# Group 0 made tile by tile in a set order with loads split over two queues, and key normalisers ahead of the next group's norm

## The chip, the cores and the metric

One core of one Trainium2 chip. The metric is the device time of one launch in microseconds (us). One profiled execution of each kernel gives a trace; a page and several views (chain of waits, timeline, windows, DMA) are read from it. "Clock" is the share of full speed that TensorE was granted, as the trace records it (1.00 is full, 0.50 half). The span of a trace is 1.8 to 1.9 us shorter than the time of its run.

## The reference, cut to what matters

```python
xn = (x - mean(x)) / sqrt(var(x) + 1e-5)                 # x: 2048 x 512
q, k, v = split(xn @ wqkv)                               # 32 heads of 16
pq, pk = q @ w_phi[h], k @ w_phi[h]                      # per head, 16 x 16
phi_q = concat(softmax(pq), softmax(-pq));  phi_k = concat(softmax(pk), softmax(-pk))
kv = sum_s phi_k[s]^T v[s];  z = sum_s phi_k[s]
A = ((phi_q @ kv) / (phi_q @ z + 1e-6)) @ wo
B = mish(xn @ w1 + b1) @ w2                              # 512 -> 1792 -> 512
out = x + A + B
```

kv is a sum over all tokens, so all keys come before any attention output. w_phi is folded into the key and query weights at the start.

## The kernel before: the parts that the change and the argument touch

The tokens run in four groups of four tiles of 128. In each group TensorE (PE) makes keys (pk), values (pv), queries (pq), seven pairs of hidden blocks (ph) and the kv sums (pkv). VectorE (DVE) sums and inverts the exponentials of the keys (ss, rk), scales the values with them (v), adds the kv sums up (kvacc), and makes the norm of the next group (st, mv, xn). ScalarE (ACT) does exponentials and Mish. POOL is GpSimd; it makes the root (rstd) of the norms after group 0. "follow" ties an instruction behind the last one of the same name in the scheduler; what is not tied, the scheduler orders. PSUM is the memory in which PE leaves its results; its buffers here are three large and two small ones, so PE waits where none is free.

```python
ps_kq = tile_pool(name="ps_kq", bufs=3, space=PSUM)   # "big": pk, pq, ph, pkv, fold
ps_v  = tile_pool(name="ps_v",  bufs=2, space=PSUM)   # pv
# ... loads, before
nc.sync.dma_start(xgs[0][:], x_g[0])
nc.scalar.dma_start(wk_raw[:], wqkv_v[:, :, D:2*D])
nc.sync.dma_start(wv[:], wqkv_v[:, :, 2*D:3*D])
nc.scalar.dma_start(Wsrc[:], wphi_v)
nc.scalar.dma_start(wq_raw[:], wqkv_v[:, :, 0:D])
# ... the norm of a group: only the statistics are tied
follow("dve", nc.vector.bn_stats(st[:], xg[:, t, :]))
nc.vector.bn_aggr(mv[:, t, :], st[:])
nc.vector.tensor_scalar(out=xn[:], in0=xg[:, t, :], ...)     # L190
nc.sync.dma_start_transpose(out=xnT[:, t], in_=xn[:])        # groups 1 to 3
# ... the loop
for g in range(NG):
    if g == 0: ...
    else:
        ek0 = k_pair(xnT, 0); ek1 = k_pair(xnT, 1)
        v0, vfin = v_pair(xnT, 0)
    vfin(ek0)                                  # ss, rk, v of tiles 0 and 1
    q_pair(g, xnT, 0); q_pair(g, xnT, 1)
    h_pair(xnT, acts[g], 0)
    v1, vfin = v_pair(xnT, 1)
    vfin(ek1)                                  # ss, rk, v of tiles 2 and 3
    if g + 1 < NG:
        xnTs[g + 1], _ = stage_ln(g + 1)       # the next group's norm
    for fp in range(1, 4): h_pair(xnT, acts[g], fp)
    stage_kvacc(g, parts)                      # 2 x pkv on PE, 2 x kvacc on DVE
    for fp in range(4, 7 if g + 1 < NG else 6): h_pair(xnT, acts[g], fp)
```

The softmax here doesn't subtract the row's maximum and nothing guards it: scores larger than these inputs give would overflow.

## Time and profile before

| | before |
|---|---|
| time, median of 3 runs | 196.7 us (196.59 to 196.71) |
| profiled run, its span | 197.05 us, 195.2 us |
| first hidden pair | 23.28 |
| keys of groups 1, 2, 3 start | 38.99, 71.03, 95.37 |
| length of group 1, group 2 | 32.04, 24.34 |
| half clock of TensorE | 53.28 to 60.11 |

All positions are us from the start of the span. Group lengths are the distance between the first key matmuls (pk) of neighbours in PE's timeline. The clock row is from the trace's records of the granted clock. Most of the lines themselves stand in the prediction; these two, for the start, do not (DVE's first look at x, and the first hidden pair; in brackets the idle time before it and what ended it):

```profile
4.59 1.29 DVE L182 BATCH_NORM_STATS2 st<-xg 128x6 f32<-128x512 bf16 x2 [3.35 <-DMA xg<-in_A_x_dram]
```
```profile
23.28 1.89 PE L366 MATMUL ph<-xnT,w_sb 128*128 128x512 bf16 x8 [0.40 <-ACT eqT L357]
```

### The profile page before, as it was taken

The page shows a single profiled execution, that of the slowest core. Times are in us where ns is not written, and L with a number is a line of the kernel's source. Part 1 is how long each engine was busy: PE and PEld are TensorE (multiplying, and loading weights), DVE is VectorE, ACT ScalarE, POOL GpSimd, SP SyncE. Part 2 cuts the span into 40 slices and gives each one's busy share as a digit, 9 for nine tenths or more (in the row PEclk, how much of TensorE's full clock was granted, in tenths as well). Part 3 has the DMA queues.
Part 4 walks back from the last instruction along what each step waited for, and adds up shares of the span by engine and source line. Part 5 has one row for each costly group of instructions (what it writes and reads, how often), then busy time and mean ns, then how long its engine had stood idle before and what let it go on. Part 6 is the DMA issues. An engine that isn't in the chain of part 4 may idle for free.

```text
span 195.2 us, 2791 instructions
## 1 busy us (share of the span) xinstructions
PE 181.2 (93%) x1034; PEld 90.7 (46%) x1051; DVE 119.0 (61%) x233; ACT 107.9 (55%) x175; POOL 14.0 (7%) x35
## 2 busy tenths in 40 slices
PE   7779999999189999999999999999999999999992
PEld 2355446444034644446444464445555555555440
DVE  1948999364894203982039864897666677766600
ACT  3578976598704479974799855343322222333311
POOL 3200410202110000110001100000000000000000
PEclk9999999999958999999999999999999999999999
DMA  6999302619300013000000000138322632222220
GB/s 192 381 403 386 151 0 55 125 59 197 108 0 0 3 27 81 0 0 3 0 0 0 0 3 0 27 81 165 55 69 66 164 81 57 54 54 57 54 81 27
DMA packets 24233, 15.93 MB, mean 82 GB/s; under 512 B 16284, under 2 KB 23196, under 8 KB 24220
## 3 DMA queue, kind: packets, MB, share of 16 engines
q1 hardware_dynamic: 22636, 14.69, 27.4%
q10 hardware_dynamic: 1584, 1.07, 1.7%
q8 instruction: 8, 0.13, 0.3%
q14 instruction: 5, 0.04, 0.1%
HBM read 9.98 MB, written 2.10 MB: 62 GB/s over the span
## 4 chain that ended last, share of the span: by engine, by line
PE 75%; ACT 7%; DVE 7%; DMA 5%; issue 2%; SPq 2%; POOL 1%; ACTq 0%; DVEq 0%; POOLq 0%
PE ph L366 25%; PE po L453 22%; PE po L462 6%; PE pv L283 6%; PE pk L265 4%; PE pkv L326 4%; DMA Wsrc<-in_A_w_phi_dram 4%; PE pq L348 4%; PE pnd L390 4%; SPq L200 2%; ACT ek L274 1%; ACT ek L273 1%; ACT act L377 1%; DMA xnT<-xn 1%; DVE ss L297 1%
## 5 line engine op out<-in xcount | busy, mean ns | idle before, releaser
L366 PE MATMUL ph<-xnT,w_sb 128*128 128x512 bf16 x224 | 51.8, 386 | 0.4 <-ACT eqT L357 0.4
L453 PE MATMUL po<-w_sb,act 128*128 128x512 bf16 x216 | 51.2, 379 | 0.4
L377 ACT ACTIVATE act<-ph,b1f 128x512 bf16<-128x512 f32 x56 | 35.5, 684 | 27.4 <-PE ph L366 27.4
L366 PEld LDWEIGHTS <-w_sb 128*128 128x128 bf16 x224 | 22.2, 100 | 27.1 <-issue 2.9
L471 ACT CAST y<-po 128x512 bf16<-128x512 f32 x16 | 9.4, 586 | 44.4 <-PE po L462 44.4
L453 PEld LDWEIGHTS <-act 128*128 128x128 bf16 x224 | 21.3, 98 | 22.3
L297 DVE TENSOR_REDUCE ss<-ek 128x64 f32<-128x1024 bf16 x16 | 18.7, 1211 | 19.1 <-ACT ek L274 19.0
L422 DVE TENSOR_TENSOR on<-pnd,wd 128x512 f32<-128x512 f32 x32 | 20.6, 686 | 1.7
L283 PE MATMUL pv<-wv,xnT 128*128 128x512 bf16 x59 | 16.4, 408 | 5.0 <-DVE v L305 4.6
L305 DVE TENSOR_TENSOR v<-pv,rk 128x1024 bf16<-128x1024 f32 x16 | 18.3, 1188 | 0.0
L462 PE MATMUL po<-wo_sb,oT 128*128 128x512 bf16 x63 | 16.4, 379 | 0.1
L357 ACT ACTIVATE eqT<-pq 128x1024 bf16<-128x1024 f32 x16 | 15.1, 1040 | 0.7 <-PE pq L348 0.6
L182 DVE BATCH_NORM_STATS2 st<-xg 128x6 f32<-128x512 bf16 x16 | 10.4, 672 | 8.1 <-DMA xg<-in_A_x_dram 8.1
L348 PE MATMUL pq<-xnT,wqp 128*128 128x512 bf16 x64 | 14.5, 379 | 0.0
L265 PE MATMUL pk<-wkp,xnT 128*128 128x512 bf16 x61 | 14.3, 379 | 0.2
L407 DVE TENSOR_TENSOR td<-ds 128x64 f32<-128x64 f32 x16 | 3.6, 225 | 16.4 <-ACT ds L403 16.3
L283 PEld LDWEIGHTS <-xnT 128*128 128x128 bf16 x64 | 6.5, 103 | 13.0 <-issue 6.6
L390 PE MATMUL pnd<-kvm,eqT 128*128 128x144 bf16 x128 | 11.3, 226 | 0.5 <-DVE on L422 0.3
L390 PEld LDWEIGHTS <-eqT 128*128 128x128 bf16 x128 | 9.0, 98 | 5.9 <-DVE on L422 2.4
L313 POOL CAST v<-rk 128x64 bf16<-128x64 f32 x16 | 7.0, 458 | 64.5 <-DVE rk L303 64.5
L429 DVE TENSOR_TENSOR o_t<-on 128x512 bf16<-128x512 f32 x16 | 11.1, 692 | 0.5
L338 DVE TENSOR_TENSOR kvacc<-pkv,kvacc 128x544 f32<-128x544 f32 x6 | 4.3, 725 | 9.9 <-PE pkv L326 9.9
(63 smaller groups left out, 150.1 us busy)
## 6 DMA issues: line engine op xcount, KB each, us to landing
xg<-in_A_x_dram SPq DMA_DIRECT2D x8, 512.0 KB, 4.1
out_dram<-y SPq DMA_DIRECT2D x16, 128.0 KB, 2.1
w_sb<-in_B_w_dram SPq DMA_DIRECT2D x2, 896.0 KB, 9.9
w_sb<-in_B_w_dram SPq DMA_DIRECT2D x1, 1792.0 KB, 12.9
wk_raw<-in_A_wqkv_dram ACTq DMA_DIRECT2D x1, 512.0 KB, 5.1
wv<-in_A_wqkv_dram SPq DMA_DIRECT2D x1, 512.0 KB, 6.0
wq_raw<-in_A_wqkv_dram ACTq DMA_DIRECT2D x1, 512.0 KB, 10.1
wo_sb<-in_A_wo_dram SPq DMA_DIRECT2D x1, 512.0 KB, 13.5
```

The source lines that it names most:

```text
L265: pe(nc.tensor.matmul(pk[:, tt, :], lhsT=xnT[:, 2 * pr + tt, kt, :], rhs=wkp[:, kt, :], start=(kt == 0), stop=(kt == KT - 1),))
L283: nc.tensor.matmul(pv[:], lhsT=xnT[:, 2 * pr + tt, kt, :], rhs=wv[:, kt, :], start=(kt == 0), stop=(kt == KT - 1),)
L297: nc.vector.reduce_sum(ss[:], ek[:, :, tt, :].rearrange("p s (h e) -> p s h e", e=DH), axis=AX.X,)
L305: nc.vector.tensor_tensor(out=v12[:, :, :, 0:DH], in0=pvs[tt][:] .rearrange("p (o h e) -> p o h e", o=1, e=DH) .to_broadcast([P, 2, NH, DH ...
L348: pe(nc.tensor.matmul(pq[:, jj, :], lhsT=wqp[:, kt, j * P : (j + 1) * P], rhs=xnT[:, :, kt, :], start=(kt == 0), stop=(kt == KT - 1),))
L357: follow("act", nc.scalar.activation(eqT[:, sl, gs], pq[:], ACT.Exp, scale=sign))
L366: nc.tensor.matmul(ph[:, ff, :], lhsT=w1_sb[:, kt, f * P : (f + 1) * P], rhs=xnT[:, :, kt, :], start=(kt == 0), stop=(kt == KT - 1),)
L377: nc.scalar.activation(act[:, f, :], ph[:, ff, :], ACT.Mish, bias=b1f[:, f : f + 1])
L390: nc.tensor.matmul(pnd[:, j // 2, (j % 2) * 144 : (j % 2) * 144 + 144], lhsT=eqT[:, pl * 4 + j, tok0 : tok0 + P], rhs=kvm[:, pl * 4 + j], ...
L422: nc.vector.tensor_tensor(out=on[:, pl], in0=nds[pl][:, :, :, 0:DH], in1=wd[:, pl, :, :, None].to_broadcast([P, 2, 16, DH]), op=ALU.mult,)
L453: nc.tensor.matmul(po[:], lhsT=acts[g][:, f, t * P : (t + 1) * P], rhs=w2_sb[:, f, :], start=False, stop=False, skip_group_check=True,)
L462: nc.tensor.matmul(po[:], lhsT=oT[:, j, :], rhs=wo_sb[:, j, :], start=False, stop=(j == 3), skip_group_check=True,)
```

## The change

Its intent: PE should never wait for v, and the ragged start should be shorter. Group 0 is written out tile by tile, with all DVE and ACT instructions tied; x and wk are split over two queues, Wsrc comes earlier, wv later; and in the loop every DVE instruction is tied in the order of the source, so the finish of the keys precedes the next group's norm. The core of the diff:

```diff
-    nc.sync.dma_start(xgs[0][:], x_g[0])
-    nc.scalar.dma_start(wk_raw[:], wqkv_v[:, :, D : 2 * D])
+    nc.sync.dma_start(xgs[0][0:H], x_g[0][0:H])              # H = 64 partitions
+    nc.scalar.dma_start(xgs[0][H:P], x_g[0][H:P])
+    nc.sync.dma_start(wk_raw[:, 0:2], wqkv_v[:, 0:2, D : 2 * D])
+    nc.scalar.dma_start(wk_raw[:, 2:4], wqkv_v[:, 2:4, D : 2 * D])
+    nc.sync.dma_start(Wsrc[:], wphi_v)                       # was on the other queue
+    nc.scalar.dma_start(wq_raw[:], ...)
+    nc.sync.dma_start(wv[:], ...)                            # was ahead of Wsrc
 ...
-                nc.vector.reduce_sum(ss[:], ...)
+                follow("dve", nc.vector.reduce_sum(ss[:], ...))
     # the same for rk, v, kvacc, bn_aggr, xn and the copy of b1f
 ...
-    xnTs[0], xns0 = stage_ln(0)
-    wkT = fold_T(wk_raw, ...)
-    ln_T(xnTs[0], xns0)
-    fold_mm(wkT, wkp)
+    n0 = Norm(0)
+    ptk, wkT = fold_T(wk_raw)
+    n0.stats(0); n0.root_act(0); n0.stats(1); n0.root_act(1)
+    for t in range(2): n0.invert(t); n0.scale(t)
+    ...                                        # cut: tiles 2 and 3, copies, fold of wk
+    pv0 = v_tile(xnTs[0], 0)
+    ...
+    ek0 = k_pair(xnTs[0], 0)                   # keys before the fold of wq
+    fold_mm(pfq, wqT, (0, 1, 2, 3))
+    ek1 = k_pair(xnTs[0], 1)
 ...
-            xnTs[g + 1], _ = stage_ln(g + 1)
+            xnTs[g + 1] = Norm(g + 1).whole()  # same place in the source, now tied on DVE
```

More of the change, by code (lines that the diff above doesn't have):

```diff
@@ L67 @@
     xgs[0] = xpool.tile([P, TPG, D], BF16, name="xg")
-    nc.sync.dma_start(xgs[0][:], x_g[0])
     wk_raw = prep_w.tile([P, KT, D], BF16, name="wk_raw")
-    nc.scalar.dma_start(wk_raw[:], wqkv_v[:, :, D : 2 * D])
+    H = P // 2
+    nc.sync.dma_start(xgs[0][0:H], x_g[0][0:H])
+    nc.scalar.dma_start(xgs[0][H:P], x_g[0][H:P])
+    nc.sync.dma_start(wk_raw[:, 0:2], wqkv_v[:, 0:2, D : 2 * D])
+    nc.scalar.dma_start(wk_raw[:, 2:4], wqkv_v[:, 2:4, D : 2 * D])
+    Wsrc = prep_w.tile([P, 4, DH], BF16, name="Wsrc")
+    with nc.allow_non_contiguous_dma(reason="tiny w_phi load"):
+        nc.sync.dma_start(Wsrc[:], wphi_v)
+    wq_raw = prep_w.tile([P, KT, D], BF16, name="wq_raw")
+    nc.scalar.dma_start(wq_raw[:], wqkv_v[:, :, 0:D])
     wv = wts.tile([P, KT, D], BF16, name="wv")
     nc.sync.dma_start(wv[:], wqkv_v[:, :, 2 * D : 3 * D])
-    Wsrc = prep_w.tile([P, 4, DH], BF16, name="Wsrc")
-    with nc.allow_non_contiguous_dma(reason="tiny w_phi load"):
-        nc.scalar.dma_start(Wsrc[:], wphi_v)
-    wq_raw = prep_w.tile([P, KT, D], BF16, name="wq_raw")
-    nc.scalar.dma_start(wq_raw[:], wqkv_v[:, :, 0:D])
     w1_sb = wts.tile([P, KT, F], BF16, name="w1_sb")
@@ L123 @@
     b1f = wts.tile([P, FT], FP32, name="b1f")
-    wqp = wts.tile([P, KT, D], BF16, name="wqp")
-    wkp = wts.tile([P, KT, D], BF16, name="wkp")
+    wqp = [wts.tile([P, 2, D], BF16, name="wqp%d" % i) for i in range(2)]
+    wkp = [wts.tile([P, 2, D], BF16, name="wkp%d" % i) for i in range(2)]
     eqT = persist.tile([P, 8, S], BF16, name="eqT")
@@ L161, in bank_v @@
         return ps_v.tile(shape or [P, 512], dt, name=name, tag="v")
-    def rstd_of(g, rstd, mv):
-        if g == 0:
-            follow("act", nc.scalar.activation(rstd, mv, ACT.Sqrt, bias=eps_t[:]))
-            nc.vector.reciprocal(rstd, rstd)
-        else:
-            nc.gpsimd.tensor_scalar(
-                out=rstd, in0=mv, scalar1=1e-5, scalar2=None, op0=ALU.add
-            )
-            nc.gpsimd.tensor_tensor(out=rstd, in0=rstd, in1=mhalf[:], op=ALU.pow)
-    def stage_ln(g):
-        xg = xgs[g]
-        mv = spool.tile([P, TPG, nc.vector.BN_AGGR_DIM], FP32, name="mv")
-        rstd = spool.tile([P, TPG], FP32, name="rstd")
-        xnT = xnTpool.tile([P, TPG, KT, P], BF16, name="xnT")
-        xns = []
-        for t in range(TPG):
-            st = spool.tile([P, nc.vector.BN_STATS_DIM], FP32, name="st")
-            follow("dve", nc.vector.bn_stats(st[:], xg[:, t, :]))
-            nc.vector.bn_aggr(mv[:, t, :], st[:])
-            if g == 0:
-                rstd_of(g, rstd[:, t : t + 1], mv[:, t : t + 1, 1])
-        if g > 0:
-            rstd_of(g, rstd[:], mv[:, :, 1])
-        for t in range(TPG):
-            xn = xnpool.tile([P, D], BF16, name="xn")
-            nc.vector.tensor_scalar(
-                out=xn[:],
-                in0=xg[:, t, :],
-                scalar1=mv[:, t, 0:1],
-                scalar2=rstd[:, t : t + 1],
-                op0=ALU.subtract,
-                op1=ALU.mult,
-            )
-            xns.append(xn)
-            if g > 0:
-                nc.sync.dma_start_transpose(out=xnT[:, t], in_=xn[:])
-        return xnT, xns
@@ L203, in ln_T, with __init__, stats, root_act @@
-    def ln_T(xnT, xns):
-        if True:
-            ptr = big("ptr", [P, TPG, KT, P], BF16)
-            for t in range(TPG):
+    class Norm:
+        def __init__(self, g):
+            self.xg = xgs[g]
+            self.mv = spool.tile([P, TPG, nc.vector.BN_AGGR_DIM], FP32, name="mv")
+            self.rstd = spool.tile([P, TPG], FP32, name="rstd")
+            self.xnT = xnTpool.tile([P, TPG, KT, P], BF16, name="xnT")
+            self.xns = {}
+        def stats(self, t):
+            st = spool.tile([P, nc.vector.BN_STATS_DIM], FP32, name="st")
+            follow("dve", nc.vector.bn_stats(st[:], self.xg[:, t, :]))
+            follow("dve", nc.vector.bn_aggr(self.mv[:, t, :], st[:]))
+        def root_act(self, t):
+            rs = self.rstd[:, t : t + 1]
+            follow(
+                "act",
+                nc.scalar.activation(rs, self.mv[:, t, 1:2], ACT.Sqrt, bias=eps_t[:]),
+            )
+        def invert(self, t):
+            rs = self.rstd[:, t : t + 1]
+            follow("dve", nc.vector.reciprocal(rs, rs))
+        def scale(self, t):
+            xn = xnpool.tile([P, D], BF16, name="xn")
+            follow(
+                "dve",
+                nc.vector.tensor_scalar(
+                    out=xn[:],
+                    in0=self.xg[:, t, :],
+                    scalar1=self.mv[:, t, 0:1],
+                    scalar2=self.rstd[:, t : t + 1],
+                    op0=ALU.subtract,
+                    op1=ALU.mult,
+                ),
+            )
+            self.xns[t] = xn
+        def turn(self, th):
+            ptr = (big if th else bank_v)("ptr", [P, 2, KT, P], BF16)
+            for t in range(2):
@@ L209, in ln_T, with whole @@
                         nc.tensor.transpose(
-                            ptr[:, t, kt, :], xns[t][:, kt * P : (kt + 1) * P], ident[:]
-                        )
-                    )
-            nc.scalar.copy(xnT[:, 0:2], ptr[:, 0:2])
-            nc.vector.tensor_copy(xnT[:, 2:4], ptr[:, 2:4])
+                            ptr[:, t, kt, :],
+                            self.xns[2 * th + t][:, kt * P : (kt + 1) * P],
+                            ident[:],
+                        )
+                    )
+            follow(
+                "dve", nc.vector.tensor_copy(self.xnT[:, 2 * th : 2 * th + 2], ptr[:])
+            )
+        def whole(self):
+            for t in range(TPG):
+                self.stats(t)
+            nc.gpsimd.tensor_scalar(
+                out=self.rstd[:],
+                in0=self.mv[:, :, 1],
+                scalar1=1e-5,
+                scalar2=None,
+                op0=ALU.add,
+            )
+            nc.gpsimd.tensor_tensor(
+                out=self.rstd[:], in0=self.rstd[:], in1=mhalf[:], op=ALU.pow
+            )
+            for t in range(TPG):
+                self.scale(t)
+                nc.sync.dma_start_transpose(out=self.xnT[:, t], in_=self.xns[t][:])
+            return self.xnT
     Wbd = prep_w.tile([P, 4, P], BF16, name="Wbd")
@@ L224, with act_copy, dve_copy, fold_T @@
         )
-    def fold_T(src, engines):
+    def act_copy(out, in_):
+        follow("act", nc.scalar.copy(out, in_))
+    def dve_copy(out, in_):
+        follow("dve", nc.vector.tensor_copy(out, in_))
+    def fold_T(src):
         ptr = big("ptrw", [P, 4, 512], BF16)
@@ L237, in fold_T, with half, fold_mm @@
                 )
-        for jh, copy in enumerate(engines):
-            ins = copy(wT[:, 2 * jh : 2 * jh + 2, :], ptr[:, 2 * jh : 2 * jh + 2, :])
-            if src is wq_raw and jh == 0:
-                follow("act", ins)
-        return wT
-    def fold_mm(wT, dst):
-        for kp in range(KT // 2):
-            pf = big("pf")
-            for kk in range(2):
-                kt = 2 * kp + kk
-                for j in range(4):
-                    pe(nc.tensor.matmul(
-                        pf[:, kk, j * P : (j + 1) * P],
+        return ptr, wT
+    def half(t, jh):
+        return t[:, 2 * jh : 2 * jh + 2, :]
+    def fold_mm(pfs, wT, js):
+        for kt in range(KT):
+            for j in js:
+                pe(
+                    nc.tensor.matmul(
+                        pfs[kt // 2][:, kt % 2, j * P : (j + 1) * P],
                         lhsT=wT[:, j, kt * P : (kt + 1) * P],
@@ L255, in fold_mm @@
                         stop=True,
-                    ))
-            follow("dve", nc.vector.tensor_copy(dst[:, 2 * kp, :], pf[:, 0]))
-            follow("act", nc.scalar.copy(dst[:, 2 * kp + 1, :], pf[:, 1]))
+                    )
+                )
     def k_pair(xnT, pr):
@@ L267, in k_pair @@
                     lhsT=xnT[:, 2 * pr + tt, kt, :],
-                    rhs=wkp[:, kt, :],
+                    rhs=wkp[kt // 2][:, kt % 2, :],
                     start=(kt == 0),
@@ L275, in k_pair, with v_tile, v_use @@
         return ek
-    def v_pair(xnT, pr):
-        pvs = []
-        for tt in range(2):
-            pv = bank_v("pv")
-            for kt in range(KT):
-                pe(
-                    nc.tensor.matmul(
-                        pv[:],
-                        lhsT=xnT[:, 2 * pr + tt, kt, :],
-                        rhs=wv[:, kt, :],
-                        start=(kt == 0),
-                        stop=(kt == KT - 1),
-                    )
-                )
-            pvs.append(pv)
+    def v_tile(xnT, t):
+        pv = bank_v("pv")
+        for kt in range(KT):
+            pe(
+                nc.tensor.matmul(
+                    pv[:],
+                    lhsT=xnT[:, t, kt, :],
+                    rhs=wv[:, kt, :],
+                    start=(kt == 0),
+                    stop=(kt == KT - 1),
+                )
+            )
+        return pv
+    def v_pair(xnT, pr):
+        return v_use([v_tile(xnT, 2 * pr + tt) for tt in range(2)])
+    def v_use(pvs):
         v12s = []
@@ L296, in finish @@
                 ss = spool.tile([P, 2, NH], FP32, name="ss")
-                nc.vector.reduce_sum(
+                follow("dve", nc.vector.reduce_sum(
                     ss[:],
@@ L300, in finish @@
                     axis=AX.X,
-                )
+                ))
                 rk = spool.tile([P, 2, NH], FP32, name="rk")
-                nc.vector.reciprocal(rk[:], ss[:])
+                follow("dve", nc.vector.reciprocal(rk[:], ss[:]))
                 v12 = vpool.tile([P, 2, NH, VW], BF16, name="v12")
-                nc.vector.tensor_tensor(
+                follow("dve", nc.vector.tensor_tensor(
                     out=v12[:, :, :, 0:DH],
@@ L311, in finish @@
                     op=ALU.mult,
-                )
+                ))
                 nc.gpsimd.tensor_copy(v12[:, :, :, DH], rk[:])
@@ L335, in stage_kvacc @@
             if g == 0:
-                nc.vector.tensor_copy(acc, src)
+                follow("dve", nc.vector.tensor_copy(acc, src))
             else:
-                nc.vector.tensor_tensor(out=acc, in0=src, in1=acc, op=ALU.add)
+                follow(
+                    "dve",
+                    nc.vector.tensor_tensor(out=acc, in0=src, in1=acc, op=ALU.add),
+                )
     def q_pair(g, xnT, jp):
@@ L349, in q_pair @@
                         pq[:, jj, :],
-                        lhsT=wqp[:, kt, j * P : (j + 1) * P],
+                        lhsT=wqp[kt // 2][:, kt % 2, j * P : (j + 1) * P],
                         rhs=xnT[:, :, kt, :],
@@ L484 @@
         )
-    xnTs[0], xns0 = stage_ln(0)
-    wkT = fold_T(wk_raw, (nc.scalar.copy, nc.scalar.copy))
-    ln_T(xnTs[0], xns0)
-    fold_mm(wkT, wkp)
-    wqT = fold_T(wq_raw, (nc.scalar.copy, nc.vector.tensor_copy))
-    follow("act", nc.scalar.activation(warm[:], eps_t[:], ACT.Exp))
+    n0 = Norm(0)
+    xnTs[0] = n0.xnT
+    ptk, wkT = fold_T(wk_raw)
+    n0.stats(0)
+    n0.root_act(0)
+    n0.stats(1)
+    n0.root_act(1)
+    for t in range(2):
+        n0.invert(t)
+        n0.scale(t)
+    act_copy(half(wkT, 0), half(ptk, 0))
+    n0.stats(2)
+    n0.root_act(2)
+    act_copy(half(wkT, 1), half(ptk, 1))
+    n0.turn(0)
+    n0.stats(3)
+    n0.root_act(3)
+    for t in range(2, 4):
+        n0.invert(t)
+        n0.scale(t)
+    pfk = [big("pf"), big("pf")]
+    fold_mm(pfk, wkT, (0, 1))
+    pv0 = v_tile(xnTs[0], 0)
+    fold_mm(pfk, wkT, (2, 3))
+    act_copy(wkp[0][:], pfk[0][:])
+    dve_copy(wkp[1][:], pfk[1][:])
+    v0, vfin = v_use([pv0, v_tile(xnTs[0], 1)])
+    n0.turn(1)
+    ptq, wqT = fold_T(wq_raw)
+    dve_copy(half(wqT, 0), half(ptq, 0))
+    dve_copy(half(wqT, 1), half(ptq, 1))
+    follow("act", nc.scalar.activation(warm[:], eps_t[:], ACT.Exp))
+    ek0 = k_pair(xnTs[0], 0)
+    pfq = [big("pf"), big("pf")]
+    fold_mm(pfq, wqT, (0, 1, 2, 3))
+    dve_copy(wqp[0][:], pfq[0][:])
+    act_copy(wqp[1][:], pfq[1][:])
+    ek1 = k_pair(xnTs[0], 1)
     for g in range(NG):
         xnT = xnTs[g]
-        if g == 0:
-            v0, vfin = v_pair(xnT, 0)
-            fold_mm(wqT, wqp)
-            ek0 = k_pair(xnT, 0)
-            ek1 = k_pair(xnT, 1)
-        else:
+        if g > 0:
             ek0 = k_pair(xnT, 0)
@@ L507 @@
             nc.tensor.transpose(pb[:], b1row[:], ident[0:FT, 0:FT])
-            nc.vector.tensor_copy(b1f[:], pb[:])
+            follow("dve", nc.vector.tensor_copy(b1f[:], pb[:]))
             prep_w.release()
```

## The prediction

> **What bounds the kernel now.** I read the page first: span 195.2 us, TensorE (PE) busy 93%. The rest of the engines have room, so time is lost only where PE waits or runs slowly. The 40 slices (4.88 us each) show where: ragged at the start (slices 0 to 2), one hole in slice 10, and a lowered granted clock in slices 11 and 12.
>
> ```profile
> PE   7779999999189999999999999999999999999992
> ...
> PEclk9999999999958999999999999999999999999999
> ```
>
> The waits view and PE's timeline name the hole: the second value projection of group 1 (the second of four token groups) waits for its PSUM bank, which VectorE (DVE) frees by writing v.
>
> ```profile
> PE pv L283 <- DVE v L305: 4.6, 1, 4.6
> ```
> ```profile
> 47.62 1.89 PE L366 MATMUL ph<-xnT,w_sb 128*128 128x512 bf16 x8
> 54.11 1.44 PE L283 MATMUL pv<-wv,xnT 128*128 128x512 bf16 x3 [4.60 <-DVE v L305]
> ```
>
> DVE's timeline shows why. It runs in order; the scheduler had put the norm of group 3 (xn, L190) ahead of the key sums (ss, L297) of group 1, and those xn wait for transposing DMAs to free their four buffers. The keys were ready at about 43.7 us (ACT's L274), yet ss begins at 49.77. Compare the undisturbed group 2: ss starts as soon as its keys are there.
>
> ```profile
> 49.44 0.41 DVE L190 TENSOR_SCALAR xn<-xg,mv,rstd 128x512 bf16<-128x512 bf16 x1 [0.88 <-DMA xnT<-xn]
> 49.77 2.34 DVE L297 TENSOR_REDUCE ss<-ek 128x64 f32<-128x1024 bf16 x2
> 52.03 0.95 DVE L303 RECIPROCAL rk<-ss 128x64 f32<-128x64 f32 x2
> 52.90 2.29 DVE L305 TENSOR_TENSOR v<-pv,rk 128x1024 bf16<-128x1024 f32 x2
> ...
> 65.11 0.72 DVE L338 TENSOR_TENSOR kvacc<-pkv,kvacc 128x544 f32<-128x544 f32 x1 [4.59 <-PE pkv L326]
> ...
> 76.26 2.35 DVE L297 TENSOR_REDUCE ss<-ek 128x64 f32<-128x1024 bf16 x2 [9.48 <-ACT ek L274]
> ```
>
> The cost of the hole: in PE's timeline group 1 starts its keys (pk) at 38.99, group 2 at 71.03, group 3 at 95.37. Group 2 takes 24.34 us without a wait, group 1 takes 32.04: 7.70 us too long. 4.60 is the wait; the other 3.1 is clock: 8 + 24 matmuls between 54.11 and 64.12 took 10.01 us instead of 32 x 0.216 = 6.91, with a granted clock of 0.50 in the windows view from 54 to 60 us.
>
> In the start, the chain of waits runs through a tiny load (Wsrc, 16 KB), POOL's Wbd, the folded weights, and ScalarE's (ACT) exponentials:
>
> ```profile
> 1.27 6.99 DMA Wsrc<-in_A_w_phi_dram
> ...
> 8.41 1.66 POOL Wbd L219 x4
> ...
> 21.40 1.84 ACT eqT L357 x2
> ```
>
> **What the Trainium skill says.** "TensorE: Matmul & The Clock Gate", Part 1 (what's actually happening): the clock falls to half after about an idle window of 3.4 us and needs a busy one to return. This trace agrees: idle from 49.5, half clock from about 53.3, full again at about 60. By that, waits under about 3 us should leave the clock alone; no run yet shows it. "Perfetto Trace Analysis", Optimization Strategy: the same bubble repeating on the engine that should be saturated can mean too few buffers for the next tile. That is what I look for below. "DMA: Bandwidth & Descriptors", Queues, rings and completion order: each DMA engine alternates between queues by packet. Before, xg (first on the one queue) landed at 4.6 and wk_raw (first on the other) at 5.9, overlapping, so xg did not have the bandwidth to itself; that fits.
>
> **The change, part by part.**
>
> *(a) Key normalisers before the next norm.* In the built order of the changed kernel, DVE in each group does: finish of keys 0 (ss, rk, v for two tiles), finish of keys 1, the norm of the next group, then the two kvacc additions. It removes the 7.70 us in group 1 outright: keys 0 ready 4.77 us after group start (43.71 and a wake-up, less 38.99), second v by about 10.6, and PE wants its bank at 10.36 + 0.86 = 11.2.
>
> *(b) What it adds: a new wait.* kvacc frees the PSUM of pkv, and PE needs those buffers for the second and third hidden pairs (ph) after the kv matmuls: three buffers serve pkv, pkv, ph, ph, ph, and the built order has waits on DVE at just these two ph. Before, kvacc ran as soon as pkv was there. Now it stands behind the whole norm. Sum on DVE from the first ss:
> - Finishing: starts 1.13 (ss), 0.435 (rk), 1.10 (v) apart, from 49.77 to 55.10 above. As rk now follows its own ss directly, and v its own rk, I add 0.11 for each of the two dependences: 2.89 a tile, 11.55 for four.
> - Statistics: four times 0.66 plus 0.17, chained and partly overlapped: 3.17.
> - POOL's root: 44.65 to 46.09 in the timeline, 1.44.
> - Four xn 1.32, first kvacc 0.72, wake-ups 0.09.
>
> Together 18.29. PE wants the buffer at 20.89 after group start (keys 95.37 - 71.03 = 24.34, less two ph pairs of 1.73).
>
> ```profile
> 88.30 2.06 PE L326 MATMUL pkv<-v,ek 128*128 128x136 bf16 x32
> 90.19 5.34 PE L366 MATMUL ph<-xnT,w_sb 128*128 128x512 bf16 x24
> 95.37 1.89 PE L265 MATMUL pk<-wkp,xnT 128*128 128x512 bf16 x7
> ```
>
> Group 1: 4.77 + 18.29 = 23.06, a wait of 2.17. Group 2: ss starts 5.23 after its start (76.26 - 71.03), so 23.52, a wait of 2.63. Group 3 has no next norm: no wait. The third ph wants its buffer 1.73 later and kvacc 0.67 later: no second wait. The transposes of xn (2.5 us to landing, issued 1.28 apart) end before the delayed keys need them.
>
> Groups 1 and 2 together: 2 x 24.34 + 4.80 = 53.5, against 95.37 - 38.99 = 56.4. **Net 2.9 us** of the 7.7.
>
> *(c) The start.* Bytes are the same; what changes is order. From the bytes per half microsecond of the windows view, 0.52 MB have moved by about 3.8 us, 1.04 MB by about 5.2. So xg, now first on both queues, lands at some 3.9 instead of 4.6, wk_raw at some 5.2 instead of 5.9. Wsrc then took 2.4 us behind wk_raw (5.9 to 8.26); the same behind the new one gives 7.5. POOL's first two Wbd (0.41 each) are there at about 8.5, so PE's order becomes:
> - eight pf to 9.0, pv tile 0 (4 x 0.216) to 9.85, eight pf to 10.4, pv tile 1 to 11.3, transposes 0.55 and 1.07 to 12.9, keys 0 (8 x 0.216) to 14.6.
> - ACT: two exponentials to 16.6, copy of wqp to 17.6; keys 1 on PE wait for DVE's wqp copy, 16.4 to 18.2; their exponentials end at 20.1 (before: 21.40); first eqT pair at 22.0.
> - The first hidden pair waits for that eqT, as before: 22.0 against 23.28, **1.3 earlier**, and the next pair at about 25.25 against 26.73, 1.5 earlier.
>
> But (b) applies to group 0 as well. DVE finishes keys 0 from 16.6 to 22.4, copies b1f, finishes keys 1 at 28.4; the norm and kvacc add 3.17 + 1.44 + 0.04 + 1.32 + 0.69 + 0.05 = 6.71: 35.1. PE would want the buffer at 25.25 + 8.80 = 34.05: a wait of 1.06. Group 1 then starts at 38.57 against 38.99: **net 0.4 us** left of 1.5.
>
> *Sum:* 0.4 + 2.9 = 3.3 us. After group 3's start the instruction order is the old one, so nothing is given back. 196.7 - 3.3 = **193.4 us**, 1.7% faster.
>
> **Rivals.**
> - *All gained.* If kvacc is not held (buffers turn another way, or the norm is shorter than I sum), the gain is 1.5 + 7.7 = 9.2 us: 187.5. For it: that is the change's intent, and PE is otherwise saturated. Against: DVE's order is fixed, and its busy sum leaves no slack between keys and kvacc. I give it 7%.
> - *The clock falls too.* Waits of 2.2 to 2.6 us recur; if they suffice to lower the clock, each costs up to 3.1 more, as in the old hole: 196 to 200, the gain gone. Against: the start has PE gaps near 1 us with a granted clock of 1.00, and the old fall came only some 3.8 us into the idle. I give it 10%.
> - *The start gains nothing.* Wsrc or wv (now behind Wsrc) may land late, as wv's 512 KB follow many small packets; then the first hidden pair keeps its old 23.3 and the new wait in group 0 makes a loss: about 194.5. Or the loads come sooner, and 0.7 more is won: 192.7.
>
> **Range and chances.** The start carries about 0.8 us of doubt, the new waits about 0.4 each in the same direction, the clock a tail upward, the first rival a tail downward. I take 191.5 to 195.4. Two per cent faster is 192.8, only 0.6 below my number: 0.33. Slower by 2% would need the clock to fall in two groups and the start to fail: 0.02.
>
> **What would show it.** Right: no wait of PE on v; in each of groups 0, 1 and 2 a PE wait for kvacc ahead of the second hidden pair after pkv (about 1.1, 2.2, 2.6 us), none in group 3; group lengths of about 26.5, 27.0 and 24.3 us; granted clock 1.00 throughout; first hidden pair at about 22.0. Wrong: kvacc starting right after pkv (first rival), slices of lowered clock after the waits (second), or the first hidden pair at 23 or later (third). A tail after group 3's start that differs from 99.8 us (195.2 - 95.37) would mean a cost that I have not seen.

## The result, and the profile after

The changed kernel took 198.99 us (median of 4 runs, 198.62 to 199.73), beside 196.64 for the kernel before on the same chip. The ratio is 1.0135, with an interval of 1.0093 to 1.0178: **1.35% slower**, within 2%, and outside the predicted range of 191.5 to 195.4. Ratios are the mean time of one kernel's fast runs over that of the other's of the same rounds, so not quite the ratio of the medians quoted.

The page's slices (4.93 us each here) have lost the hole of slice 10. Counting from 0, smaller dips stand in its place in slices 7, 12 and 18, and the clock is lowered in slices 1 and 2 and in slice 19.

```profile
PE   7598999799995999994999999999999999999993
...
PEclk9789999999999999999799999999999999999999
```

The waits view (line waited for: us in total, times, longest) names the new releasers. It lists no wait of PE on v any more. A small one stays in group 2, hidden in a merged line: the fifth matmul of the second pv starts 0.45 us after the fourth instead of 0.22, at 79.38, when v has just ended at 79.32.

```profile
PE ph L397 <- DVE kvacc L368: 5.7, 2, 3.0
...
PE ptrw L261 <- DMA wk_raw<-in_A_wqkv_dram: 1.9, 1, 1.9
PE ph L397 <- DVE kvacc L364: 1.4, 1, 1.4
```

PE's timeline (start us, us, what, in brackets the idle time before it and what ended it) shows one such wait in each of groups 0, 1 and 2:

```profile
37.25 3.61 PE L397 MATMUL ph<-xnT,w_sb 128*128 128x512 bf16 x16 [1.39 <-DVE kvacc L364]
...
64.47 3.61 PE L397 MATMUL ph<-xnT,w_sb 128*128 128x512 bf16 x16 [2.71 <-DVE kvacc L368]
...
87.31 1.89 PE L397 MATMUL ph<-xnT,w_sb 128*128 128x512 bf16 x8
92.15 5.30 PE L397 MATMUL ph<-xnT,w_sb 128*128 128x512 bf16 x16 [2.95 <-DVE kvacc L368]
97.29 3.62 PE L290 MATMUL pk<-wkp,xnT 128*128 128x512 bf16 x16
```

Compare the second and fourth line here: the same 16 matmuls took 3.61 us in group 1 and 5.30 in group 2. DVE's timeline of group 2 shows what the pair waits for: the last v, then the whole norm with its trip to POOL, then kvacc.

```profile
84.18 1.23 DVE L333 TENSOR_TENSOR v<-pv,rk 128x1024 bf16<-128x1024 f32 x1
85.32 0.68 DVE L177 BATCH_NORM_STATS2 st<-xg 128x6 f32<-128x512 bf16 x1
...
90.09 1.38 DVE L195 TENSOR_SCALAR xn<-xg,mv,rstd 128x512 bf16<-128x512 bf16 x4 [1.48 <-POOL rstd L231]
91.38 1.34 DVE L368 TENSOR_TENSOR kvacc<-pkv,kvacc 128x544 f32<-128x544 f32 x2
```

The windows view (stretch and its length, then busy us and count of PE, weight load, DVE, ACT and POOL, then granted clock, DMA share, GB/s) shows why group 2 was slower: after the wait the clock was at half for 3.4 us.

```profile
85.00:93.20 8.20, 5.25 (x48) 3.33 (x47) 6.11 (x15) 2.69 (x5) 1.27 (x2) 1.00 0.10 20
93.20:96.60 3.40, 3.40 (x9) 1.18 (x8) 0.00 (x0) 1.27 (x2) 0.00 (x0) 0.50 0.55 110
96.60:100.00 3.40, 3.40 (x17) 1.57 (x16) 0.00 (x0) 2.02 (x3) 0.00 (x0) 1.00 0.41 154
```

In this profile the start is no shorter. x was ready on DVE at 5.36 (before: 4.59), the first weight transposes ran at 7.09 (before: 5.90), and the first hidden pair at 23.67 (before: 23.28).

```profile
5.36 0.69 DVE L177 BATCH_NORM_STATS2 st<-xg 128x6 f32<-128x512 bf16 x1 [4.11 <-DMA xg<-in_A_x_dram]
```
```profile
7.09 1.22 PE L261 MATMUL ptrw<-ident,wk_raw 128*128 128x128 bf16 x16 [1.92 <-DMA wk_raw<-in_A_wqkv_dram]
...
9.42 1.03 PE L276 MATMUL pf<-Wbd,wT 128*128 128x128 bf16 x8 [0.25 <-ACT wT L250]
...
23.67 1.89 PE L397 MATMUL ph<-xnT,w_sb 128*128 128x512 bf16 x8
```

| us from the start of the span | before | predicted | after |
|---|---|---|---|
| x ready on DVE | 4.59 | 3.9 | 5.36 |
| first hidden pair | 23.28 | 22.0 | 23.67 |
| keys of group 1 start | 38.99 | 38.57 | 40.70 |
| length of group 1 | 32.04 | 26.5 | 27.22 |
| length of group 2 | 24.34 | 27.0 | 29.37 |
| group 3's start to the end | 99.8 | 99.8 | 99.9 |
| span | 195.2 | 191.9 | 197.2 |

### The profile page after: what moved, and what is told of

The parts are those of the page before. It is cut to its first block, busy times and chain, and to the rows that moved or that the text cites. A ratio compares the mean times of both kernels' runs of the same rounds, so it can differ in the third digit from the quotient of the medians.

```text
span 197.2 us, 2802 instructions
## 1 busy us (share of the span) xinstructions
PE 181.7 (92%) x1051; PEld 91.2 (46%) x1051; DVE 125.1 (63%) x233; ACT 105.8 (54%) x171; POOL 14.3 (7%) x35
## 3 DMA queue, kind: packets, MB, share of 16 engines
q10 hardware_dynamic: 880, 1.05, 1.9%
## 4 chain that ended last, share of the span: by engine, by line
PE 57%; DVE 29%; ACT 6%; DMA 3%; issue 2%; POOL 2%; SPq 0%; DVEq 0%; ACTq 0%
PE po L484 22%; PE ph L397 13%; DVE v L333 7%; DVE ss L325 6%; PE po L493 6%; PE pk L290 5%; DVE st L177 4%; PE pnd L421 3%; DVE rk L331 3%; DMA wk_raw<-in_A_wqkv_dram 3%; PE pv L306 2%; DVE xn L195 2%; PE pq L379 2%; POOL rstd L231 2%; ACT ek L299 1%
## 5 line engine op out<-in xcount | busy, mean ns | idle before, releaser
L397 PE MATMUL ph<-xnT,w_sb 128*128 128x512 bf16 x224 | 52.6, 388 | 7.1 <-DVE kvacc L368 5.7
L484 PE MATMUL po<-w_sb,act 128*128 128x512 bf16 x224 | 51.8, 379 | 0.0
L325 DVE TENSOR_REDUCE ss<-ek 128x64 f32<-128x1024 bf16 x16 | 19.4, 1211 | 25.8 <-ACT ek L299 25.8
L333 DVE TENSOR_TENSOR v<-pv,rk 128x1024 bf16<-128x1024 f32 x16 | 19.6, 1227 | 1.7 <-PE pv L306 0.2
L478 ACT CAST po<-xg 128x512 f32<-128x512 bf16 x16 | 10.0, 624 | 1.2 <-DVE v L333 1.0
L434 ACT COPY ds<-pnd 128x64 f32<-128x64 f32 x32 | 8.7, 280 | 3.0 <-PE pnd L421 3.0
```

The lines of the kernel that those rows point to most:

```text
L325: follow("dve", nc.vector.reduce_sum(ss[:], ek[:, :, tt, :].rearrange("p s (h e) -> p s h e", e=DH), axis=AX.X,))
L333: follow("dve", nc.vector.tensor_tensor(out=v12[:, :, :, 0:DH], in0=pvs[tt][:] .rearrange("p (o h e) -> p o h e", o=1, e=DH) .to_broadcast ...
L397: nc.tensor.matmul(ph[:, ff, :], lhsT=w1_sb[:, kt, f * P : (f + 1) * P], rhs=xnT[:, :, kt, :], start=(kt == 0), stop=(kt == KT - 1),)
L484: nc.tensor.matmul(po[:], lhsT=acts[g][:, f, t * P : (t + 1) * P], rhs=w2_sb[:, f, :], start=False, stop=False, skip_group_check=True,)
```

## The experiments

All twelve kernels gave correct results. Three batches ran; the runs of one batch shared a chip and the runs of the kernel before, whose medians were 196.39, 196.21 and 196.31 (196.64 in the measurement of the change). A difference between kernels of two batches is one of medians, so some 0.4 us of it can be the batch. "Slow" runs (a few, named below) are in the medians but not in the ratios. My theory: the time is lost where kvacc stands behind the norm (PE's new wait), in the lowered clock that such a wait can bring, and in the way the loads were split. Rivals: the tied start, or the tied order of the loop as such.

### 1. kvacc inside the norm

The changed kernel with kvacc between the next group's statistics and its xn.

```diff
-            xnTs[g + 1] = Norm(g + 1).whole()
+            nxt = Norm(g + 1); nxt.whole_stats()       # statistics and POOL's root
         for fp in range(1, 4): h_pair(xnT, acts[g], fp)
         stage_kvacc(g, parts)
+        if g + 1 < NG: xnTs[g + 1] = nxt.whole_scale() # xn and its transposes
```

> The changed kernel with one thing moved: on VectorE the two kvacc additions stand after the next norm's statistics and before its xn, while POOL works out the root. Theory (kvacc held behind the norm is the new wait): the waits of PE on kvacc of 1.55, 2.88 and 3.11 us (gaps before the second hidden pair after pkv) fall below 0.3 each; the norm's xn then end up to 0.7 us later relative to the keys, so waits of up to 1.5 us a group on the transposes of xn may appear in their place; no lowered clock in groups 0 to 2. Time about 194 us (192 to 195.5). Rival (the waits are something else, kvacc only seems to be named): gaps and time stay, 198 to 200 us.

Measured: 192.16 us (191.8 to 192.52), ratio 0.9783 [0.9732, 0.9835]: 6.8 us below the changed kernel, and 2.2% below the kernel before. It fell in the theory's range. No PE wait on kvacc is left. In PE's waits a smaller one takes its place, since xn is now later and its transposing DMAs are not done when the next keys want them:

```profile
PE pk L296 <- DMA xnT<-xn: 1.5, 6, 0.3
```

Groups 1 and 2 took 24.93 and 25.38 us instead of 27.22 and 29.37. So the hold of kvacc, with what followed from it, was the larger part of the loss.

### 2. Old loads

The changed kernel with the loads in the old order and unsplit (x whole on the one queue, wk whole on the other, then wv and Wsrc, then wq).

> The changed kernel with the loads of the kernel before (x whole on one queue first, wk_raw whole on the other, Wsrc behind it). Theory (the halves on two queues made x and wk_raw land later, not sooner, and the longer idle of PE lowered the clock in the start): x lands at about 4.6 and wk_raw at about 5.9 again (instead of 5.36 and 7.08), the clock stays 1.00 in the first 15 us, the first hidden pair starts at 22.3 to 22.9 instead of 23.67. Time 0.8 to 1.5 us less than the changed kernel: 197.5 to 198.2, less a chance of 1.7 where no wait lowers the clock. Rival (the loads do nothing, the set order of the start is itself slow): first hidden pair stays at 23.5 or later, time 199.

Measured: 197.97 us (196.12 to 199.66; 2 of 10 runs slow), ratio 1.0063 [1.0018, 1.0108]. As the theory had it, the first hidden pair is at 22.51 instead of 23.67. The medians differ by 1.0 us from the changed kernel; at the same clock of 0.991 it is some 0.7 (197.9 to 198.4 against 198.62 and 198.90). The runs also fall in levels: with a mean clock of 1.00 they took 196.1 to 196.2, with 0.991 197.9 to 198.4. That pointed at the clock.

### 3. The loop's order alone

The kernel before, with its own start and loads; only the DVE instructions of the loop are tied as in the change.

```diff
-                nc.vector.reduce_sum(ss[:], ...)
+                follow("dve", nc.vector.reduce_sum(ss[:], ...))
     # the same for rk, v, kvacc, b1f; bn_aggr and xn where g > 0
```

> The kernel before with only the VectorE order in the loop of the changed kernel (finish of keys, then next norm, then kvacc), its old start. Theory (the loop's order gives back nearly all it wins): no wait on v in group 1, but waits on kvacc of about 3.0, 2.9 and 2.9 us in groups 0, 1, 2, with the clock falling in at least one of them; group 1 starts at about 42 us instead of 38.99; time 197.5 to 200. Rival (my prediction's sizes; the start of the changed kernel does the harm): 193 to 195 us.

Measured: 200.19 us (199.55 to 201.69), ratio 1.0203 [1.0136, 1.027]. The waits on kvacc are 3.04, 2.67 and 2.95 us in groups 0, 1 and 2, and group 1 starts its keys at 41.75 instead of 38.99. So the order of the loop by itself loses 3.8 us, though it removes a hole of 7.7: it takes one away and puts in three. The time is just above the theory's range.

### 4. The start alone

The changed kernel's start and loads, with the loop's DVE instructions free as before.

> The changed kernel's start, with VectorE free in the loop as before (the scheduler again puts the norms early). Theory (the new start is worth about nothing or a little less): first hidden pair at 23.3 to 23.8, group 1 starts at 39.0 to 39.6, the wait on v of 4 to 5 us with its half clock is back in group 1, time 196.5 to 197.5, that is within 0.5 us of the kernel before. Rival (the new start is worth what I predicted, 1.3 to 1.5 us): 195.2 to 195.5.

Measured: 194.98 us (194.02 to 197.67; 1 of 16 runs slow), ratio 0.9917 [0.9892, 0.9942]. My expectation (no better than 196.5) missed, and the rival's (195.2 to 195.5) is passed too. The first hidden pair is at 22.96 here, with the start and the loads of the changed kernel (23.67), and group 1 starts 0.54 us earlier than in the kernel before. The rest is the old hole: here the wait on v is 3.91 us and half clock follows for one window of 3.41 us, where the profile of before had two. Of before's 25 runs in this batch 14 had a mean clock of 0.982 to 0.983 and 9 had 0.991; of these 16 all but the slow one had 0.990 or 0.991.

### 5. The norm at the beginning of the group

As experiment 1, but in groups 1 and 2 the whole norm of the next group goes ahead of the finish of the keys, where DVE idles and waits for ACT. x is loaded one group earlier for it.

```diff
             v0, vfin = v_pair(xnT, 0)
+        if 0 < g < NG - 1: xnTs[g + 1] = Norm(g + 1).whole()
         vfin(ek0)
```

> The changed kernel, but the norm of the next group is moved from behind the finish of the keys to the very beginning of groups 1 and 2, where VectorE idles (7.3 us before the first key sum in the run that put kvacc inside the norm); group 0 stays as in that run. Theory (the wait is nothing but VectorE's order, and VectorE has the room): no PE wait on kvacc and none on the transposes in groups 1 and 2, so both take 24.3 us (that run: 24.93 and 25.38), pk starts near 39.4 / 63.9 / 88.2, time 190.2 to 191.2, about 1.5 us below that run's 192.2. Rival (VectorE is full from the first key on, and 6 us more in front of the keys push the finish of keys and so v late): a PE wait on v of 1 to 3 us in groups 1 and 2, and no gain against 192.2.

Measured: 190.12 us (190.07 to 190.38), ratio 0.9685 [0.9638, 0.9732]. It is 0.1 us below the theory's range. From the kv sums on, group 1 of this kernel runs without a gap, and group 2 starts where it should:

```profile
56.26 2.06 PE L360 MATMUL pkv<-v,ek 128*128 128x136 bf16 x32
...
63.34 3.62 PE L296 MATMUL pk<-wkp,xnT 128*128 128x512 bf16 x15
...
74.79 1.02 PE L312 MATMUL pv<-wv,xnT 128*128 128x512 bf16 x4 [0.29 <-DVE v L339]
```

What the rival expected came too, but as 0.29 us, not 1 to 3. Groups 1 and 2 took 24.89 and 24.57 us, close to the 24.34 of a group without a wait.

### 6. The same with the old loads

The edit of experiment 5 with the loads of experiment 2.

> The run before this one, with the loads in their old order: x whole on the one queue, wk whole on the other, then wv and Wsrc, wq. Theory (the two halves by partitions do not run side by side, which makes x and wk land later and leaves PE idle long enough for half clock in the start): first hidden pair about 1.1 us earlier (22.5 to 22.9 against 23.7), no half clock in the first 20 us, time about 1 us below the run before: 189.1 to 190.2. Rival (the load order only shifts slack, the start hangs on the exponentials): within 0.3 us of the run before.

Measured: 189.39 us (189.25 to 189.43), ratio 0.9644 [0.9598, 0.969]; first hidden pair at 22.47 (experiment 5: 22.96). The theory's range held. With the full clock in both, the old loads are 0.7 us better than the split by halves, and no run of one reaches a run of the other.

### 7. x split by token tiles, not by partitions

The changed kernel with one edit:

```diff
-    nc.sync.dma_start(xgs[0][0:H], x_g[0][0:H])
-    nc.scalar.dma_start(xgs[0][H:P], x_g[0][H:P])
+    nc.sync.dma_start(xgs[0][:, 0:2], x_g[0][:, 0:2])
+    nc.scalar.dma_start(xgs[0][:, 2:4], x_g[0][:, 2:4])
```

> The changed kernel with one edit: x of group 0 is split over the two queues by token tiles (all 128 partitions on each queue, packets of 2 KB) instead of by halves of the partitions (64 each, packets of 4 KB). Everything else as in the changed kernel. Theory ([...]the two halves run one after the other): with all partitions on each queue both halves run at once; x complete at about 4.5 us instead of 5.36, wk at 5.9 to 6.4 instead of 7.08, first hidden pair 0.5 to 1 us earlier than 23.67, time 198.0 to 198.6 against 199.0. Rival (two queues share what there is, or 2 KB packets cost as much as is won; or the late landing comes from wk's split and the early Wsrc): x at 5 us or later, time within 0.3 us of 199.0.

Measured: 198.95 us (198.39 to 199.8), ratio 1.0136 [1.0076, 1.0195]. The time is the rival's; the mechanism is the theory's. DVE's and PE's timelines of this kernel:

```profile
4.20 0.69 DVE L177 BATCH_NORM_STATS2 st<-xg 128x6 f32<-128x512 bf16 x1 [2.96 <-DMA xg<-in_A_x_dram]
```
```profile
5.49 1.27 PE L261 MATMUL ptrw<-ident,wk_raw 128*128 128x128 bf16 x16 [0.17 <-DMA wk_raw<-in_A_wqkv_dram]
...
22.56 1.67 PE L397 MATMUL ph<-xnT,w_sb 128*128 128x512 bf16 x7
...
63.36 5.00 PE L397 MATMUL ph<-xnT,w_sb 128*128 128x512 bf16 x16 [2.71 <-DVE kvacc L368]
```

In these two profiles x is there 1.16 us earlier than with the halves, wk 1.6 earlier, the first hidden pair 1.11 earlier. The packets are smaller as well (2 KB instead of 4), but that is not the cause: x whole, in packets of 4 KB, was there at 4.42 to 4.59 in five profiles. But the last line has 5.00 us where the changed kernel had 3.61: in this run the clock fell after the wait of group 1 as well, and the gain was gone.

### 8. More dummy matmuls in the start

Experiment 5 with 18 instead of 10 dummy matmuls before wk_raw lands.

> The first run of this batch with 18 instead of 10 dummy matmuls ahead of the first transposes, so that PE has no hole until wk_raw lands at about 7.1 us. Theory (the hole of 1.9 us before wk_raw plus the transposes brings the half clock at 7.9 to 11.3 us, and it costs some of the start): granted clock 1.00 throughout the first 20 us, the first eight pf in 0.45 to 0.6 us instead of 1.03, first hidden pair 0.2 to 0.8 us earlier than in the first run, time down by the same. Rival (the start hangs on ACT and VectorE behind Wsrc, PE's half clock is hidden): first hidden pair and time within 0.2 us; or the dummies, when the loads come early, hold up the transposes and it is slower.

Measured: 190.12 us (190.01 to 190.48), ratio 0.9688. No difference, as the rival had it. It settles little about the clock, which had not fallen in the start of experiment 5 either. But the profiles together settle what half clock in the start costs. Six have the loads by halves. From the first transposes of wk to the first hidden pair, the two with half clock there took 16.58 and 16.55 us (the changed kernel and experiment 1), the four without 16.09 to 16.13 (experiments 4, 5, 8 and 10). So it costs some 0.45 us. Experiment 10, whose wk came at nearly the same time as in the changed kernel (7.09, then 23.67), shows it best:

```profile
7.11 1.07 PE L261 MATMUL ptrw<-ident,wk_raw 128*128 128x128 bf16 x16 [1.72 <-DMA wk_raw<-in_A_wqkv_dram]
...
23.20 1.89 PE L397 MATMUL ph<-xnT,w_sb 128*128 128x512 bf16 x8
```

### 9 and 10. TensorE kept busy in the three waits

Dummy matmuls behind the first hidden pair after the kv sums, in groups 0 to 2: in experiment 9 on the kernel of experiment 7, in experiment 10 on the changed kernel itself.

```diff
         for fp in range(4, 7 if g + 1 < NG else 6):
             h_pair(xnT, acts[g], fp)
+            if fp == 4 and g + 1 < NG:
+                for _ in range((6, 11, 12)[g]):
+                    nc.tensor.matmul(pz[:], lhsT=zero[:, 0:P], rhs=zero[:], ...)
```

> The changed kernel with x split by token tiles (measured 198.95; first hidden pair 22.56, waits on kvacc 1.39 / 2.71 / 2.9, half clock right after the waits of groups 1 and 2 in its profile), and dummy matmuls of TensorE put into the three waits for kvacc: 6, 11 and 12 of 128x512 (0.216 us each: 1.3, 2.4, 2.6 us), behind the first hidden pair that follows the kv matmuls. The wait of the second pair stays the same, since VectorE sets it; only TensorE is not idle in it. Theory (the idle of the wait is what lowers the clock): granted clock 1.00 in groups 1 and 2, the 16 ph behind each wait take 3.61 us where they took 5.00 and 5.30, time 195.5 to 196.3. Rival (the lowered clock is chance or load, not idleness): half clock comes as before, time 198.5 to 199.5.

> The changed kernel itself with the same 6, 11 and 12 dummy matmuls in its three waits for kvacc, nothing else changed. Theory (idle lowers the clock): the half clock after the wait of group 2 goes, 1.9 us of its length with it (1.69 and 0.23); the cold window in the start may stay, since the dummies do not touch it; time 196.8 to 197.5 against 199.0. Rival (chance): 198.6 to 199.7.

Measured: experiment 9 195.98 us (195.43 to 200.6; 1 of 14 runs slow), ratio 0.9985 [0.9959, 1.0012]; experiment 10 196.93 us (196.55 to 199.25, 22 runs), ratio 1.0045 [1.0023, 1.0067]. Both in the theory's range: 3.0 us below experiment 7 and 2.1 below the changed kernel. The wait for kvacc is as long as before, but the clock stays up. Windows view of experiment 10, to be held against that of the changed kernel above:

```profile
85.00:93.20 8.20, 7.84 (x61) 4.48 (x60) 5.64 (x14) 2.53 (x4) 1.26 (x2) 1.00 0.16 33
93.20:96.60 3.40, 3.40 (x17) 1.55 (x16) 0.00 (x0) 2.53 (x4) 0.00 (x0) 1.00 0.48 91
```

and PE's timeline of experiment 10, the dummies and the 16 matmuls after them:

```profile
88.56 2.75 PE L593 MATMUL pz<-zero 128*128 128x512 bf16 x12
91.68 3.61 PE L397 MATMUL ph<-xnT,w_sb 128*128 128x512 bf16 x16 [0.36 <-DVE kvacc L368]
```

So in the loop it is the idle of the wait that lowers the clock, not chance and not load. Not all of the 2.1 us is the filling's: between the two profiles group 2 is 1.69 us shorter (29.37 and 27.68), and 0.47 is the start, whose clock happened to stay up and which the dummies do not touch. 21 of the 22 runs of experiment 10 had a mean clock of 0.997 or more; the changed kernel's four had 0.983 or 0.991.

### 11. Both edits together

Experiment 5 with x split by token tiles.

> The best of both: the norm of the next group at the beginning of groups 1 and 2, and x of group 0 split by token tiles instead of by partition halves (x at 4.2 instead of 5.4, wk at 5.4 instead of 6.8 in the runs so far). Theory (the order of VectorE and the way of the split are separate costs that add): first hidden pair 22.5, no wait on kvacc, time 189.0 to 189.6, about 0.8 us below the same with halves (190.1) and equal to the old loads (189.4). Rival (start gained at x is lost behind wv, which landed late with the tile split): 189.7 to 190.3.

Measured: 189.64 us (188.81 to 192.29; 1 of 6 runs slow, the 192.29), ratio 0.9637 [0.96, 0.9674]. The median is 0.04 above the theory's range; the ratio is that of experiment 6 (0.9644). First hidden pair at 22.52. The rival was right in part: with this split wv lands late, and what x gains is partly lost in the wait for it. Experiment 9 has the same start. These are the first pv of experiment 11 and of experiment 9:

```profile
9.61 1.02 PE L312 MATMUL pv<-wv,xnT 128*128 128x512 bf16 x4 [0.88 <-DMA wv<-in_A_wqkv_dram]
```
```profile
9.07 1.02 PE L306 MATMUL pv<-wv,xnT 128*128 128x512 bf16 x4 [0.25 <-DMA wv<-in_A_wqkv_dram]
```

Experiment 9 begins it 0.54 us earlier, and its first hidden pair is 0.54 earlier too (21.98). An earlier wv was not tried. **Experiments 6 and 11 are the best versions, 3.6% faster than the kernel before.**

### 12. The early norm on the kernel before

The kernel before with its own start and loads, all loop instructions of DVE tied, and the norm placed as in experiment 5.

> The kernel before with its own start and its own loads; only VectorE's loop order is set: finish of keys 0, finish of keys 1, kvacc, with the next group's norm at the beginning of groups 1 and 2 (in group 0 its statistics ahead of kvacc, its scaling behind). So nothing of the change but the idea, without the norm between finish and kvacc. Theory (the hole of group 1 is worth its 7.7 us when nothing is put in its place): first hidden pair 23.3, group 1 starts about 39, groups 1 and 2 take 24.4 each, time 189.8 to 190.8, 6 us below before. Rival (the old start leaves VectorE late in group 0, as when order alone was set: group 1 at 41.75): 192 to 193.5.

Measured: 192.73 us (191.95 to 193.98), ratio 0.9808 [0.9765, 0.9851]. The time is the rival's, but not for its reason: group 1 did not start at 41.75 but at 39.6. It then lost 1.24 us in four waits for the transposes of group 0's late xn (39.62 to 43.64 in PE's timeline), and half of the runs had one window of half clock (193.3 to 194.0 at a clock of 0.991, against 191.95 to 192.12 at 0.997 or 1.00). So once the loop no longer holds PE, the new start is worth 2.0 us with the halves and 2.5 with the tile split (192.1 against 190.1 and 189.6, at full clock).

### When the clock falls

In every trace the clock changes on a grid of 3.41 us. I laid this grid over PE's timeline and added up PE's idle time in each window. In the loop (leaving out the start, where transposes run):

| kernel | window | PE idle in it | next window |
|---|---|---|---|
| before | 49.87 to 53.28 | 3.41 | half clock |
| changed | 89.77 to 93.19 | 2.38 | half clock |
| experiment 7 | 90.08 to 93.50 | 2.35 | half clock |
| experiment 2 | 61.00 to 64.41 | 2.31 | half clock |
| experiment 4 | 50.72 to 54.13 | 2.17 | half clock |
| experiment 7 | 59.36 to 62.78 | 2.13 | half clock |
| experiment 3 | 91.10 to 94.51 | 2.10 | half clock |
| changed | 62.47 to 65.88 | 2.00 | full |
| experiment 2 | 88.30 to 91.72 | 1.99 | full |
| experiment 3 | 36.48 to 39.90 | 1.82 | full |

No window with more than 2.05 us idle was followed by full clock in the loop of any trace, none with less by half clock, save that before's half clock lasted a second window with 1.05 us idle in the first. The limit is read from these runs alone, and lies between the 2.00 and the 2.10 of the table. So a wait of 2.5 to 3.1 us brings half clock or not by where it falls in the grid, and the grid lies differently in each run. That is why group 1 of the changed kernel kept its clock (its 2.88 us of idle were cut into 0.88 and 2.00) and group 2 did not, and why the runs of one kernel fall into levels. A window of half clock cost 1.69 us in group 2.

## Why the prediction was wrong

In the loop its mechanism was right: the hole of group 1 went, and kvacc behind the norm made a new wait in groups 0, 1 and 2, none in group 3, with the tail as before. Two other steps failed, the landing of x in the start and the clock after the waits. Both showed by its own signs of being wrong: the first hidden pair at 23 or later, and slices of lowered clock after the waits. The sum was wrong by 5.3 us of span (197.2 against 191.9), and these are the terms.

- **The start, "1.3 earlier" (1.67 us wrong).** This step failed. It took the bytes per half microsecond of before as given and only changed their order, so "xg, now first on both queues, lands at some 3.9". The halves by 64 partitions hardly ran side by side. The DMA view (queue, KB each, us from issue to landing) of the changed kernel:

```profile
xg<-in_A_x_dram ACTq DMA_DIRECT2D x1, 256.0 KB, 3.2
```

  Both halves were issued at 0.79; ACT's landed at 4.0, and DVE began on x at 5.36. In the trace's packet records the 64 packets of ACT's half begin between 2.12 and 3.21 us, those of the other half between 3.03 and 4.08. In experiment 7 both queues' packets of x begin together, from 1.82 and from 2.04. In the windows view from 3.5 to 5 us the changed kernel moved 210 GB/s where before and experiment 7 moved 352 and 351. The Trainium skill says it on the page "SBUF — State Buffer", section "Can I just issue two DMAs to hit both halves?": to reach all ports a transfer must span all 128 partitions, and two transfers on the two halves together brought 6% over one. I had not looked there. The trace shows the order in time; the ports it doesn't show. All fourteen profiles agree:

| x loaded | profiles | x ready on DVE | first hidden pair |
|---|---|---|---|
| halves by partitions | changed, 1, 4, 5, 8, 10 | 5.36 to 6.05 | 22.96 to 23.90 |
| whole, the new start | 2, 6 | 4.42 to 4.49 | 22.47 to 22.51 |
| by token tiles | 7, 9, 11 | 4.13 to 4.38 | 21.98 to 22.56 |
| whole, the old start | before, 3, 12 | 4.44 to 4.59 | 23.03 to 23.29 |

  The late x holds up what is queued behind it, Wsrc too: POOL began on Wbd at 8.65 to 9.31 us with the halves, and at 6.61 to 7.62 with the tiles. In the four profiles of the halves with full clock in the start, the first pf waits for Wbd (0.55 to 0.67 us), so the third rival (Wsrc lands late) was right in part; in the changed kernel's own profile it waits for ACT's copy of wk. The 1.67 us are that profile's. By experiment 8, some 0.47 of them are half clock in the start, and the other 1.2 the way of loading. Split by tiles, the start can be what was predicted (21.98 for 22.0, experiment 9).
- **The rival "The clock falls too", given 10% (1.69 us in this profile's group 2; 1.39 + 1.69 in the two groups of experiment 7's).** This step failed as well. "By that, waits under about 3 us should leave the clock alone" did not hold: 2.10 us of idle within one window was enough. The evidence against, "the old fall came only some 3.8 us into the idle", was misread: the whole window before that fall was idle, so it said nothing on how little suffices. Filling the waits gave the 1.69 us of group 2 back (experiment 10).
- **The waits, 1.06, 2.17 and 2.63 us (0.5, 0.7 and 0.5 us too small).** The mechanism was right, two terms mis-sized. A finish of keys took 3.04 us a tile instead of 2.89 (four from 45.45 to 57.6 in group 1), and the statistics 3.28 instead of 3.17: 4 x 0.15 + 0.11 = 0.71, which is the miss of group 1. The gaps in PE's timeline, from the end of one pair (start plus 8 x 0.216) to the start of the next, were 1.55, 2.88 and 3.11.
- **The rest, some 0.2 us**, is the small wait on v that group 2 keeps.
- **Range and chances.** The range added the doubts of the steps as if the clock were a tail. The mean clock below 1.00 in all four runs shows that it was the rule.

Experiment 9 checks the sum: there the start is as predicted and the clock full, so only the waits (1.7) and the small wait on v (0.2) should be left. Its span is 193.8 against 191.9. In time, its 195.98 is 2.6 us above 193.4: these 1.9, and 0.35 because I took the gain from the median of before while its profile was of a run of 197.05; the rest is scatter of runs.

Open: why the clock fell in the start of the changed kernel (7.85 to 11.27). There 1.93 us of idle, with transposes after it, came ahead of half clock, and 2.43 in experiment 1, while 1.72 us, with more transposes, did not in experiment 10. Its cost is the 0.45 us of experiment 8.

## What to carry to other kernels

A fixed order that takes one wait away can make another: list, for each buffer that the bounding engine reuses, what stands ahead of the instruction that frees it, and put long work that nobody waits for yet (here the next norm) where its engine idles, not ahead of a release. Count a wait of the tensor engine with the clock it may cost after it, and suspect the clock where the runs of one kernel fall into levels. When one tensor is split over two queues, split along the free dimension, so that each half keeps all partitions, and look at what then lands last (here wv). Take a difference of under 1 us in the start from more than one profile: the same start had its first hidden pair anywhere from 22.96 to 23.90.

## What the Trainium skill lacked or had wrong

- "TensorE: Matmul & The Clock Gate", Part 1 and the table under "Why this matters for your kernels" speak of an idle window of 3.4 us and of gaps over about 3 us. The grid and its length agree (3.41 us, free-running), but a window need not be wholly idle: in the loop 2.10 to 2.38 us of idle in one window (six cases) lowered the clock, 2.00 and less did not. A gap of about 2.5 us can do it.
- The same page asks for one busy window for the return, and doesn't say how busy. Nine windows of half clock with 0.00 to 0.59 us of idle were followed by full clock; the one with 1.05 us of idle (before, from 53.28) by a second window of half clock.
- "SBUF — State Buffer", "Can I just issue two DMAs to hit both halves?" was right for halves of the partitions (x at 5.36 to 6.05 instead of 4.42 to 4.59). It doesn't say what two transfers do that each span all 128 partitions: x was there at 4.13 to 4.38.
